# First four token tiles brought in by a transposing DMA and centred after it, in a fused layer-norm, linear-attention and gated feed-forward kernel

## The chip, the cores and the metric

The kernel runs on one core of one Trainium2 chip. The metric is the device time of one execution in microseconds; where several runs are given, their median is meant. The profile comes from one further execution, recorded by the hardware profiler. Its span goes from the first to the last instruction.

The engines are named as in the profile: PE is TensorE's matmul, PEld its weight load, DVE VectorE, ACT ScalarE, POOL GpSimd, SP SyncE. SP and ACT issue the DMAs here; the queue of SP is q1 in the profile, that of ACT is q10. 16 DMA engines serve both.

## The reference

```
x  = A_x                                   # 1 x 2048 x 640, bfloat16
xn = (x - mean(x)) / sqrt(var(x) + 1e-5)   # over the 640 columns of a token
q, k, v = split(xn @ wqkv)                 # 32 heads of 20
phi(t) = where(t > 0, t + 1, exp(t)) + 1e-6
kv  = sum over tokens of phi(k) v^T ;  z = sum over tokens of phi(k)
s   = (phi(q) kv / (phi(q) z + 1e-6)) @ wo
g   = silu(relu(xn @ w1) @ w2)             # 640 -> 1728 -> 640
out = x + s * g
```

## The kernel before, in words

The 2048 tokens are 16 tiles of 128 tokens (t = 0 to 15), or four chunks of 512 (j = 0 to 3). The 640 columns are five blocks of 128 (C = 5). A product needs its input with the columns on the partitions, so every tile of x has to be transposed. For tiles 4 to 15 that is done after the normalisation: `LN_norm` (line 487) writes the normalised tile `xn`, and `xnT_dma` (line 545) transposes it from SBUF to SBUF by a DMA of SP. Tiles 0 to 3 open the kernel and don't wait for their variance: they are only centred, transposed on TensorE, copied from PSUM into `xcT`, and multiplied; the factor 1/sqrt(var + eps) (`rsy`) is applied afterwards, as the scale of the exp and relu that empty the K products (`K_evac`, line 566).

The order of the head is written out by hand, from line 689 to line 743. Each call there appends instructions to the list of its engine, and every engine works through its own list in order. A small scheduler (`Sched`) derives the waits from what each instruction reads and writes. So an instruction that waits holds up everything behind it on its engine, whatever else is ready. The parts that matter here:

- `x_load`, `w_load`, `w1_load`, `wk_load` (lines 372 to 398) issue the loads; lines 405 to 421 are their order. x tile 0, the k part of wqkv (`wk`, five blocks of 128 rows in four loads), w1 and x tiles 4 to 7 are issued by SP, x tiles 1 to 3 by ACT.
- `fill(32)` (line 436) runs 32 products of ones with ones on TensorE from the start, `fill(5)` (line 697) five more. Their results are not used.
- `bn` (line 467) takes the statistics of half a tile on VectorE; `aggr` (line 472) joins two halves into mean and variance on VectorE, then adds eps and raises to -0.5 on POOL.
- For tiles 0 to 3 the mean comes earlier: for tiles 0 and 3 half from VectorE's half statistics (`half_mean_dve`, line 502) and half from ScalarE's accumulator (`mean_act`, line 507), for tiles 1 and 2 wholly from ScalarE. `centre` (line 514) subtracts it on VectorE, `transposes` (line 527) runs five 128x128 transposes on TensorE, and `xcT_copy` (line 534) moves the result from PSUM to `xcT` in two pieces, by VectorE or ScalarE.
- `K_mm` (line 551, matmuls at line 556) multiplies a tile of `xcT` or `xnT` by `wk`, ten matmuls of 128x320 for a tile, into two PSUM banks. `K_exp` and `K_relu` (lines 573 and 576, both at line 569) empty them on ScalarE with the scale `rsy`.
- After the four K tiles, `H_block(0, f)` for f = 4, 5, 10, 11, 12 (line 1102) multiplies blocks of w1 by all four tiles of `xcT`, five matmuls of 128x512 each (line 658), into the banks 2 to 6 in turn. The first two of these banks are those that `K_exp(0)` and `K_relu(0)` empty. Between these blocks VectorE takes the statistics of tiles 5 to 7 and normalises tiles 4 to 7.
- Then come the K products of tiles 4 to 7, the other H blocks and Q products, and a long stretch of products in Strassen form up to the output (helpers `seven` and `h_unit`, matmuls at lines 882 and 1036). None of it is touched.

Of the kernel before, what the change touches and what calls it, by code (L numbers as in the profile page):

```python
# [208 lines left out]
def bass_recurrent_scan__linear_attn_block__dense_activation_relu__prompt_kernel(  # L209
# [159 lines left out]
    def xs(t):  # L369
        return t if t < XR else (t - 4) % XR  # L370
# [20 lines left out]
    def w1_load(d0, d1, E, extra=()):  # L391
        for d in range(d0, d1):
            w_load(w1_p[d], B_w1[:, WL[d]:WL[d + 1]], ("w1", d), E=E, extra=extra)

    def wk_load(k0, k1):
        dma("SP", lambda eng: eng.dma_start(wk[:, k0:k1, :],
                                            A_wqkv[P * k0:P * k1, D:2 * D].rearrange("(c p) n -> p c n", p=P)),
            W=[("wk", k) for k in range(k0, k1)])

# [2 lines left out]
    sc.op("ACT", lambda eng: eng.activation(out=msum[:, 3, 0:1], in_=zero[:, 0:1], func=ACTF.Copy),  # L402
          R=[("zero",)], W=[("msum", 3, 0)])
    sc.allow_unread.add(("msum", 3, 0))
    x_load(0)
    x_load(1, 1, "ACT")
    wk_load(0, 1)
    x_load(2, 1, "ACT")
    wk_load(1, 2)
    x_load(3, 1, "ACT")  # L410
    wk_load(2, 3)
    wk_load(3, 5)
    w1_load(2, 3, "SP")
    w1_load(5, 6, "SP")
    x_load(4)
    x_load(5)
    w1_load(6, NW, "SP")
    x_load(6)
    x_load(7)
# [13 lines left out]
                        for _ in range(n)], W=[("ps", 7)])  # L433

    sc.allow_unread.add(("ps", 7))
    fill(32)

    def build_consts():
        sc.op("POOL", lambda eng: eng.memset(sel[:, :], 1.0 / 32), W=[("sel",)])
# [32 lines left out]
    def aggr(t):  # L472
# [12 lines left out]
    last_norm = [None]  # L485

    def LN_norm(t):
        if t >= 99:
            sc.op("POOL", lambda eng: eng.scalar_tensor_tensor(
                out=rsv[:, t:t + 1], in0=mv[:, t, 0:1], scalar=-1.0, in1=rsy[:, t:t + 1], op0=ALU.mult, op1=ALU.mult),  # L490
                R=[("mv", t), ("rsy", t)], W=[("rsv", t)])
            last_norm[0] = sc.op("ACT", lambda eng: eng.activation(
                out=xn[:, t, :], in_=xin[:, xs(t), :], func=ACTF.Identity, bias=rsv[:, t:t + 1],
                scale=rsy[:, t:t + 1]), R=[("xin", xs(t)), ("rsv", t), ("rsy", t)], W=[("xn", t)])
            xnT_dma(t)
            return
        last_norm[0] = sc.op("DVE", lambda eng: eng.tensor_scalar(
            out=xn[:, t, :], in0=xin[:, xs(t), :], scalar1=mv[:, t, 0:1], scalar2=rsy[:, t:t + 1],
            op0=ALU.subtract, op1=ALU.mult), R=[("xin", xs(t)), ("mv", t), ("rsy", t)], W=[("xn", t)])
        xnT_dma(t)  # L500

    def half_mean_dve(t):
        sc.op("DVE", lambda eng: eng.tensor_scalar(out=msum[:, t, 0:1], in0=stats[:, t, 0, 1:2],
                                                   scalar1=stats[:, t, 0, 4:5], scalar2=0.25, op0=ALU.add, op1=ALU.mult),
              R=[("stats", t, 0)], W=[("msum", t, 0)])

    def mean_act(t, lo):
        junk = ek[:, eks(t), 0, 0:D - lo]
        sc.op("ACT", lambda eng: eng.activation(out=junk, in_=xin[:, xs(t), lo:D], func=ACTF.Copy, scale=1.0 / D,
                                                accum_out=msum[:, t, 1:2]),  # L510
              R=[("xin", xs(t))], W=[("msum", t, 1), ("ek_e", eks(t))])
        sc.allow_unread.add(("ek_e", eks(t)))

    def centre(t):
        split = ((0, P * TS), (P * TS, D)) if t == 0 else ((0, D),)
        for part, (c0, c1) in enumerate(split):
            key = ("xn", t, 0) if t == 0 and part == 0 else ("xn", t)
            if t in (1, 2):
                sc.op("DVE", lambda eng, c0=c0, c1=c1: eng.tensor_scalar(
                    out=xn[:, t, c0:c1], in0=xin[:, t, c0:c1], scalar1=msum[:, t, 1:2], scalar2=None,  # L520
                    op0=ALU.subtract), R=[("xin", t), ("msum", t, 1)], W=[key])
            else:
                sc.op("DVE", lambda eng, c0=c0, c1=c1: eng.tensor_scalar(
                    out=xn[:, t, c0:c1], in0=xin[:, t, c0:c1], scalar1=msum[:, t, 0:1], scalar2=msum[:, t, 1:2],
                    op0=ALU.subtract, op1=ALU.subtract), R=[("xin", t), ("msum", t, 0), ("msum", t, 1)], W=[key])

    def transposes(t, b):
        for part, (c0, c1) in enumerate(((0, TS), (TS, C))):
            psb = ps[b + part].bitcast(bf)
            sc.group("PE", [(lambda eng, c=c, c0=c0, psb=psb: eng.transpose(  # L530
                psb[:, P * (c - c0):P * (c - c0 + 1)], xn[:, t, P * c:P * (c + 1)], ident[:])) for c in range(c0, c1)],
                R=[("xn", t, 0) if t == part == 0 else ("xn", t), ("ident",)], W=[("ps", b + part)])

    def xcT_copy(t, b, part, E):
        psb = ps[b + part].bitcast(bf)
        c0, c1 = (0, TS) if part == 0 else (TS, C)
        dst = xcT[:, c0:c1, tok(t)]
        src = psb[:, 0:P * (c1 - c0)].rearrange("p (c q) -> p c q", c=c1 - c0)
        if E == "DVE":
            sc.op("DVE", lambda eng: eng.tensor_copy(dst, src), R=[("ps", b + part)], W=[("xcT", t, part)])  # L540
        else:
            sc.op("ACT", lambda eng: eng.activation(out=dst, in_=src, func=ACTF.Copy), R=[("ps", b + part)],
                  W=[("xcT", t, part)])

    def xnT_dma(t):
        dma("SP", lambda eng: eng.dma_start_transpose(
# [139 lines left out]

    bn(0, 0)
    mean_act(0, HN)  # L690
    half_mean_dve(0)
    centre(0)
    mean_act(1, 0)
    transposes(0, 0)
    xcT_copy(0, 0, 0, "DVE")
    centre(1)
    fill(5)
    K_mm(0, 2, 0, 1)
    transposes(1, 6)
    xcT_copy(0, 0, 1, "DVE")  # L700
    mean_act(2, 0)
    xcT_copy(1, 6, 0, "DVE")
    bn(0, 1)
    xcT_copy(1, 6, 1, "ACT")
    K_mm(0, 2, 1, KA)
    K_mm(1, 4, 0, KA)
    K_mm(0, 2, 2, 3)
    centre(2)
    transposes(2, 0)
    mean_act(3, HN)  # L710
    bn(3, 0)
    xcT_copy(2, 0, 0, "DVE")
    xcT_copy(2, 0, 1, "ACT")
    half_mean_dve(3)
    centre(3)
    aggr(0)
    bn(2, 0)
    K_mm(1, 4, 2, 3)
    K_mm(2, 6, 0, KA)
    K_mm(2, 6, 2, 3)  # L720
    transposes(3, 0)
    bn(1, 0)
    xcT_copy(3, 0, 0, "DVE")
    xcT_copy(3, 0, 1, "ACT")
    bn(1, 1)
    aggr(1)
    K_mm(0, 2, 3, C)
    K_mm(1, 4, 3, C)
    bn(2, 1)
    aggr(2)  # L730
    K_exp(0, 2)
    K_relu(0, 2)
    K_mm(2, 6, 3, C)
    K_mm(3, 0)
    K_exp(1, 4)
    K_relu(1, 4)
# [960 lines left out]
```

## Time and profile before

| | us |
|---|---|
| median of 3 runs (lowest to highest) | 208.31 (208.11 to 208.32) |
| span of the profiled execution | 207.0 |
| the runs' median less that span | 1.3 |
| TensorE busy | 203.6 |
| VectorE busy | 169.7 |
| ScalarE busy | 124.3 |
| POOL busy | 18.0 |
| first matmul of the H blocks in the chain | 12.58 |

The page gives no time for the profiled execution but its span. How to read what follows: the page's first section gives for each engine its busy time, its share of the span and its instructions; the fourth the chain of work that ended last, followed back from the last instruction. The trace answers further questions: the chain in order of time, the instructions of a stretch in order of time, the busy time of each engine in given stretches, one source line's instructions, and for the DMAs the bytes that each queue moved in a stretch and the time from an issue to the landing of its last byte.

The loads of the head, issue to landing, by that last view: x tile 0 is issued by SP at 0.80 us and needs 2.5 us; x tile 1, by ACT at 0.97 us, 2.7 us; the last load of `wk` (320 KB), by SP at 2.68 us, 5.2 us; the first w1 loads (320 KB each), by SP from 3.16 us, 6.1 us.

### The profile page before, as it was taken

Reading aid. Unit: us, or ns where it says so; the run is one execution under the profiler, and the core shown is the slowest. Engines: PE = TensorE matmul, PEld = TensorE weight load, DVE = VectorE, ACT = ScalarE, POOL = GpSimd, SP = SyncE. Lnnn points to the kernel's source line nnn. Section 1 sums busy time; section 2 is a strip of 40 time slices with the busy share of each in tenths; the row PEclk is TensorE's granted clock in tenths of the full one; section 3 lists DMA queues with packets and bytes.
Section 4 is the critical chain, followed back from the end, with each engine's and each line's share of the span. In section 5 each row is a group of like instructions: output and inputs, shape, how many; then the busy total and the mean of one; then the engine's idle time right before and its main releaser. Section 6 shows DMA issues by size and latency. Waiting matters only on the chain.

```text
span 207.0 us, 3745 instructions
## 1 busy us (share of the span) xinstructions
PE 203.6 (98%) x1400; PEld 126.3 (61%) x1400; DVE 169.7 (82%) x373; ACT 124.3 (60%) x251; POOL 18.0 (9%) x53
## 2 busy tenths in 40 slices
PE   8999999999999999999999999999999999999995
PEld 7755645545555444444456777777777777777773
DVE  4888997988969787686889669898888989897465
ACT  5598869888889987686563435462525354352531
POOL 3174032101330000000000000000000000000001
PEclk9999999999999999999999999999999999999999
DMA  6965999211037000302225999237931011010103
GB/s 194 331 190 117 255 203 275 42 32 29 6 63 198 25 3 0 127 0 57 74 63 114 251 357 384 90 108 234 371 129 63 3 63 46 21 63 0 63 5 127
DMA packets 32999, 24.74 MB, mean 119 GB/s; under 512 B 12757, under 2 KB 32981, under 8 KB 32981
## 3 DMA queue, kind: packets, MB, share of 16 engines
q1 hardware_dynamic: 31749, 23.13, 39.2%
q10 hardware_dynamic: 1232, 1.37, 1.9%
q8 instruction: 11, 0.18, 0.4%
q14 instruction: 7, 0.06, 0.1%
HBM read 15.81 MB, written 5.24 MB: 102 GB/s over the span
## 4 chain that ended last, share of the span: by engine, by line
PE 97%; DMA 1%; DVE 1%; issue 0%
PE psT L882 40%; PE psT L1036 19%; PE psT L556 11%; PE psT L609 11%; PE psT L658 6%; PE psT L1529 3%; PE psT L1580 2%; DMA reg<-in_A_x_dram 1%; PE psT L676 1%; PE psT L1320 1%; PE psT L530 1%; PE psT L1294 1%; PE psT L756 1%; PE psT L786 1%; PE psT L432 0%; DVE stats L469 0%
## 5 line engine op out<-in xcount | busy, mean ns | idle before, releaser
L882 PE MATMUL psT<-reg,regH 128*128 128x320 bf16 (+1 forms) x224 | 34.3, 299 | 0.0
L882 PE MATMUL psT<-reg 128*128 128x320 bf16 (+1 forms) x164 | 27.7, 299 | 0.0
L882 PEld LDWEIGHTS psT<-reg,regH 128*128 128x128 bf16 (+1 forms) x224 | 21.9, 98 | 8.6
L1354 ACT ACTIVATE wv_sb<-psT 128x320 bf16<-128x320 f32 x28 | 11.3, 436 | 25.2 <-PE psT L882 15.4
L609 PE MATMUL psT<-reg 128*128 128x512 bf16 x100 | 24.4, 379 | 0.0
L1036 PE MATMUL psT<-reg 128*128 128x512 bf16 x80 | 23.2, 379 | 0.0
L827 DVE TENSOR_TENSOR psT<-psT,reg 128x320 f32<-128x320 f32 x30 | 14.3, 493 | 9.3 <-PE psT L882 9.2
L889 ACT ACTIVATE psT<-psT 128x320 f32<-128x320 f32 x32 | 13.6, 426 | 11.2 <-PE psT L882 10.7
L882 PEld LDWEIGHTS psT<-reg 128*128 128x128 f16 (+1 forms) x164 | 16.0, 98 | 6.9 <-DVE regH L827 0.2
L889 ACT ACTIVATE reg<-psT 128x320 f32<-128x320 f32 (+1 forms) x24 | 10.4, 435 | 15.6 <-PE psT L882 13.6
L556 PE MATMUL psT<-reg 128*128 128x320 bf16 x120 | 17.9, 299 | 0.0
L1042 ACT ACTIVATE psT<-psT 128x512 f32<-128x512 f32 x20 | 11.9, 595 | 8.2 <-PE psT L1036 8.2
L569 ACT ACTIVATE regE<-psT 128x640 bf16<-128x640 f32 x24 | 15.6, 706 | 1.9 <-PE psT L556 1.2
L609 PEld LDWEIGHTS psT<-reg 128*128 128x128 bf16 x100 | 9.6, 98 | 11.6 <-issue 0.7
L1048 ACT ACTIVATE regH<-psT 128x512 bf16<-128x512 f32 (+1 forms) x24 | 14.5, 604 | 2.1 <-PE psT L1036 1.8
L556 PEld LDWEIGHTS psT<-reg 128*128 128x128 bf16 x120 | 11.5, 98 | 6.5 <-ACT regE L569 0.5
L469 DVE BATCH_NORM_STATS2 stats<-reg 128x6 f32<-128x320 bf16 x32 | 14.1, 475 | 1.3 <-DMA reg<-in_A_x_dram 1.3
L827 DVE TENSOR_TENSOR reg<-reg 128x1024 f16<-128x1024 bf16 (+6 forms) x17 | 13.5, 805 | 1.7 <-DMA reg<-in_B_w_dram 1.2
L882 PE MATMUL psT<-reg,pqT 128*128 128x320 bf16 (+1 forms) x72 | 14.7, 299 | 0.0
L1517 DVE TENSOR_TENSOR reg<-psT,wv_sb 128x640 bf16<-128x640 f32 (+2 forms) x16 | 11.8, 739 | 3.0 <-PE psT L882 1.8
L1036 PEld LDWEIGHTS psT<-reg 128*128 128x128 bf16 x80 | 7.7, 98 | 9.4 <-issue 0.4
L1522 POOL TENSOR_TENSOR reg<-reg 128x224 bf16<-128x224 bf16 x1 | 0.6, 607 | 144.0 <-DVE reg L1517 144.0
(143 smaller groups left out, 369.0 us busy)
## 6 DMA issues: line engine op xcount, KB each, us to landing
reg<-in_B_w_dram SPq DMA_DIRECT2D x12, 320.0 KB, 5.5
scr<-rden SPq DMA_DIRECT2D x4, 640.0 KB, 8.3
reg<-in_A_x_dram SPq DMA_DIRECT2D x4, 640.0 KB, 6.6
out_dram<-reg SPq DMA_DIRECT2D x15, 160.0 KB, 1.9
regE<-scr SPq DMA_DIRECT2D x3, 640.0 KB, 7.5
reg<-in_A_x_dram SPq DMA_DIRECT2D x4, 320.0 KB, 4.4
reg<-in_A_wo_dram SPq DMA_DIRECT2D x6, 160.0 KB, 3.3
reg<-in_A_x_dram SPq DMA_DIRECT2D x5, 160.0 KB, 5.5
```

The lines of the kernel that those rows point to most:

```text
L469: sc.op("DVE", lambda eng: eng.bn_stats(stats[:, t, a, :], xv[:, HN * a:HN * (a + 1)]), R=[("xin", xs(t))], W=[("stats", t, a)])
L556: fns.append(lambda eng, a=a, k=k, lhs=lhs: eng.matmul(ps[b + a][:, 0:HN], lhsT=lhs, rhs=wk[:, k, HN * a:HN * (a + 1)], start=(k == 0), st ...
L569: sc.op("ACT", lambda eng: eng.activation(out=o_.rearrange("p (a n) -> p a n", a=2), in_=ps2(b, HN), func=func, scale=scale), R=[("ps", b) ...
L609: sc.group("PE", [(lambda eng, k=k: eng.matmul(ps[b], lhsT=wq[:, k, P * f:P * (f + 1)], rhs=xnT[:, j, k, :], start=(k == 0), stop=(k == C ...
L658: sc.group("PE", [(lambda eng, k=k: eng.matmul(ps[b], lhsT=w1_col(k, P * f, P), rhs=src[:, k, :], start=(k == 0), stop=(k == C - 1))) for ...
L827: sc.op("DVE", lambda eng: eng.tensor_tensor(out=out, in0=in0, in1=in1, op=op), R=R, W=W, extra=extra)
L882: sc.group("PE", [(lambda eng, k=k, lhs=lhs, rhs=rhs: eng.matmul(ps[b][:, 0:HN], lhsT=lhs, rhs=rhs, start=(start and k == 0), stop=(k == n ...
L889: sc.op("ACT", lambda eng: eng.activation(out=dst, in_=ps[b][:, 0:HN], func=ACTF.Copy), R=[("ps", b)], W=[dkey], extra=extra)
L1036: sc.group("PE", [(lambda eng, k=k, lhs=lhs, rhs=rhs: eng.matmul(ps[b], lhsT=lhs, rhs=rhs, start=(start and k == 0), stop=(k == n - 1), sk ...
L1042: sc.op("ACT", lambda eng: eng.activation(out=dst, in_=ps[b], func=ACTF.Copy), R=[("ps", b)], W=[dkey], extra=extra)
L1048: sc.op("ACT", lambda eng: eng.activation(out=dst, in_=ps[b], func=ACTF.Relu), R=[("ps", b)], W=[("hT", j, f)])
L1517: sc.op("DVE", lambda eng: eng.tensor_tensor(out=tmpo[:, os_, lo:hi].rearrange(shp, a=na), in0=src, in1=g_of(t)[0][:, lo:hi].rearrange(shp ...
```

## The change

The raw tiles 0 to 3 of x come twice. Once they come by a DMA that transposes on the way, straight from DRAM into `xcT` (`xT_load`, issued by SP ahead of all else); once as before into `xin`, for the statistics and the later normalisation. On the transposed tile the mean of a token is a sum over partitions: `sums` multiplies ones by the five blocks, so that each row of the PSUM tile holds the token sums, and the new `centre` subtracts sum/640 on VectorE, in place, in two pieces. The transposes, the copies and the early means of before are gone. The variances of tiles 0 and 1 move to ScalarE (`act_stats`: a pass for the mean, a pass of squares); those of tiles 2 and 3 stay with VectorE. ACT now issues all loads of `wk` and of x tiles 0 to 3, the last two in one; on SP, x tiles 4 and 5 go ahead of a w1 block. The fillers are 29 and 3.

```diff
-    def wk_load(k0, k1):
-        dma("SP", lambda eng: eng.dma_start(wk[:, k0:k1, :],
+    def wk_load(k0, k1, E="SP"):
+        dma(E, lambda eng: eng.dma_start(wk[:, k0:k1, :],
...
-    x_load(0)
+    def xT_load(t):
+        dma("SP", lambda eng: eng.dma_start_transpose(xcT[:, :, tok(t)], x2[tok(t), :]), W=[("xr", t)])
+
+    for t in range(4):
+        xT_load(t)
+    wk_load(0, 1, "ACT")
+    wk_load(1, 2, "ACT")
+    wk_load(2, 3, "ACT")
+    wk_load(3, 5, "ACT")
+    x_load(0, 1, "ACT")
     x_load(1, 1, "ACT")
-    wk_load(0, 1)
-    x_load(2, 1, "ACT")
-    wk_load(1, 2)
-    x_load(3, 1, "ACT")
-    wk_load(2, 3)
-    wk_load(3, 5)
+    x_load(2, 2, "ACT")
     w1_load(2, 3, "SP")
-    w1_load(5, 6, "SP")
     x_load(4)
     x_load(5)
+    w1_load(5, 6, "SP")
     w1_load(6, NW, "SP")
...
-    fill(32)
+    fill(29)
...
+    def act_stats(t):
+        junk = ek[:, eks(t), 0, :]
+        key = ("ek_e", eks(t))
+        sc.allow_unread.add(key)
+        sc.op("ACT", lambda eng: eng.activation(out=junk, in_=xin[:, t, :], func=ACTF.Copy, scale=-1.0 / D,
+                                                accum_out=msum[:, t, 0:1]), R=[("xin", t)], W=[("msum", t, 0), key])
+        sc.op("ACT", lambda eng: eng.activation(out=junk, in_=xin[:, t, :], func=ACTF.Square, bias=msum[:, t, 0:1],
+                                                accum_out=msum[:, t, 1:2]),
+              R=[("xin", t), ("msum", t, 0)], W=[("msum", t, 1), key])
+        sc.op("POOL", lambda eng: eng.tensor_scalar(out=rsv[:, t:t + 1], in0=msum[:, t, 1:2], scalar1=1.0 / D,
+                                                    scalar2=EPS_LN, op0=ALU.mult, op1=ALU.add),
+              R=[("msum", t, 1)], W=[("rsv", t)])
...
-        if t >= 99:
...
+        if t < NA:
+            last_norm[0] = sc.op("DVE", lambda eng: eng.tensor_scalar(
+                out=xn[:, t, :], in0=xin[:, t, :], scalar1=msum[:, t, 0:1], scalar2=rsy[:, t:t + 1],
+                op0=ALU.add, op1=ALU.mult), R=[("xin", t), ("msum", t, 0), ("rsy", t)], W=[("xn", t)])
...
+    def sums(t, b):
+        sc.group("PE", [(lambda eng, c=c: eng.matmul(ps[b][:, 0:P], lhsT=one, rhs=xcT[:, c, tok(t)],
+                                                     start=(c == 0), stop=(c == C - 1))) for c in range(C)],
+                 R=[("xr", t)], W=[("ps", b)])
+
+    def centre(t, b, part):
         c0, c1 = (0, TS) if part == 0 else (TS, C)
...
+        o_ = xcT[:, c0:c1, tok(t)]
+        sc.op("DVE", lambda eng: eng.scalar_tensor_tensor(
+            out=o_, in0=ps[b][:, 0:P].unsqueeze(1).to_broadcast([P, c1 - c0, P]), scalar=-1.0 / D, in1=o_,
+            op0=ALU.mult, op1=ALU.add), R=[("ps", b), ("xr", t)], W=[("xcT", t, part)])
```

`NA` is 2. The head's order before is lines 689 to 733 above; after the change it reads, up to the K products of tile 3 and from there on as before:

```
    sums(0, 0)
    centre(0, 0, 0)
    centre(0, 0, 1)
    fill(3)
    act_stats(0)
    K_mm(0, 2, 0, KA)
    K_mm(0, 2, 2, 3)
    sums(1, 1)
    centre(1, 1, 0)
    centre(1, 1, 1)
    K_mm(0, 2, 3, C)
    act_stats(1)
    K_mm(1, 4, 0, KA)
    sums(2, 0)
    bn(2, 0)
    centre(2, 0, 0)
    centre(2, 0, 1)
    K_mm(1, 4, KA, C)
    K_exp(0, 2)
    K_relu(0, 2)
    bn(2, 1)
    K_mm(2, 6, 0, KA)
    sums(3, 1)
    centre(3, 1, 0)
    centre(3, 1, 1)
    K_mm(2, 6, KA, C)
    aggr(2)
    bn(3, 0)
    K_mm(3, 0)
```

More of the change, by code (lines that the diff above doesn't have):

```diff
@@ L379, in w_load @@
         dma(E, lambda eng: eng.dma_start(dst, src.rearrange("(c p) n -> p c n", p=P)), W=[key], extra=extra)
+    NA = 2
     KA = 2
@@ L478, in aggr @@
                                                     op=ALU.pow), R=[("rsv", t), ("mhalf",)], W=[("rsy", t)])
+    def act_stats(t):
[10 more added lines that the diff above has]
+              R=[("msum", t, 1)], W=[("rsv", t)])
+        sc.op("POOL", lambda eng: eng.tensor_tensor(out=rsy[:, t:t + 1], in0=rsv[:, t:t + 1], in1=mhalf[:, :],
+                                                    op=ALU.pow), R=[("rsv", t), ("mhalf",)], W=[("rsy", t)])
     def LN_stats(t):
@@ L487, in LN_norm @@
     def LN_norm(t):
-        if t >= 99:
[L489 to L494, printed above, removed]
+        if t < NA:
+            last_norm[0] = sc.op("DVE", lambda eng: eng.tensor_scalar(
+                out=xn[:, t, :], in0=xin[:, t, :], scalar1=msum[:, t, 0:1], scalar2=rsy[:, t:t + 1],
+                op0=ALU.add, op1=ALU.mult), R=[("xin", t), ("msum", t, 0), ("rsy", t)], W=[("xn", t)])
             xnT_dma(t)
@@ L500, in LN_norm @@
         xnT_dma(t)
[L502 to L535, printed above, removed]
-        c0, c1 = (0, TS) if part == 0 else (TS, C)
[L537 to L543, printed above, removed]
+    def sums(t, b):
+        sc.group("PE", [(lambda eng, c=c: eng.matmul(ps[b][:, 0:P], lhsT=one, rhs=xcT[:, c, tok(t)],
+                                                     start=(c == 0), stop=(c == C - 1))) for c in range(C)],
+                 R=[("xr", t)], W=[("ps", b)])
@@ L685, in H_half @@
         return a
[L689 to L705, printed above, removed]
-    K_mm(1, 4, 0, KA)
[L707 to L716, printed above, removed]
-    bn(2, 0)
[L718 to L730, printed above, removed]
+    sums(0, 0)
[4 more added lines that the diff above has]
+    K_mm(0, 2, 0, KA)
+    K_mm(0, 2, 2, 3)
+    sums(1, 1)
+    centre(1, 1, 0)
+    centre(1, 1, 1)
+    K_mm(0, 2, 3, C)
+    act_stats(1)
+    K_mm(1, 4, 0, KA)
+    sums(2, 0)
+    bn(2, 0)
+    centre(2, 0, 0)
+    centre(2, 0, 1)
+    K_mm(1, 4, KA, C)
     K_exp(0, 2)
     K_relu(0, 2)
-    K_mm(2, 6, 3, C)
+    bn(2, 1)
+    K_mm(2, 6, 0, KA)
+    sums(3, 1)
+    centre(3, 1, 0)
+    centre(3, 1, 1)
+    K_mm(2, 6, KA, C)
+    aggr(2)
+    bn(3, 0)
     K_mm(3, 0)
```

## The prediction, made before the changed kernel was run

> **What bounds the kernel now.** I read the page first: shares by engine, then the chain that ended last.
>
> ```profile
> PE 203.6 (98%) x1400; PEld 126.3 (61%) x1400; DVE 169.7 (82%) x373; ACT 124.3 (60%) x251; POOL 18.0 (9%) x53
> ...
> PE 97%; DMA 1%; DVE 1%; issue 0%
> ```
>
> TensorE is busy 98% of the span and is 97% of the chain; the rest lies at the two ends. So whatever shifts the first unbroken stretch of TensorE work shifts the end by the same amount, unless a later wait swallows it. The change touches only the head, so the second view is the chain in order of time, 0 to 40 us (columns: start, length, what):
>
> ```profile
> 0.80 2.48 DMA reg<-in_A_x_dram
> ...
> 4.49 0.79 PE psT L530 x5
> 5.28 0.53 PE psT L432 x5
> 5.81 0.52 PE psT L556 x2
> 6.33 0.28 PE psT L530 x5
> 6.61 1.21 PE psT L556 x8
> ...
> 9.59 2.99 PE psT L556 x22
> 12.58 5.40 PE psT L658 x25
> ```
>
> From 4.49 us TensorE never stops: transposes (L530), filler (L432), K products (L556), and at 12.58 the first H products (L658). The mark to compare is that **12.58**. The K products before 6.2 us take 0.26 us each, later 0.15 and 0.136 us: the array is at half rate until about 6.2 us (the 32 fillers, 0.84 to 4.41 us, give 0.112 us each, against 0.056 for the transposes at 6.33). The clock column below shows 1.00 there too; I go by the durations.
>
> Third, what the transfers do meanwhile: stretches of 1 us (last two columns: DMA share, GB/s) and the queues in 3 to 4 us (packets, MB, share):
>
> ```profile
> 3.00:4.00 1.00, 1.00 (x13) 1.00 (x11) 0.66 (x2) 0.70 (x3) 0.15 (x1) 1.00 0.99 341
> 7.00:8.00 1.00, 1.00 (x12) 0.81 (x11) 0.89 (x4) 0.68 (x3) 0.00 (x0) 1.00 1.15 339
> ```
>
> ```profile
> q1 hardware_dynamic: 147, 0.17, 50.8%
> q10 hardware_dynamic: 153, 0.17, 48.5%
> ```
>
> The DMA engines are **full** from 2 us on: two queues together move 341 GB/s, one alone 339. So an early byte that is added delays every later byte, and moving loads to ACT's queue (q10) buys no rate. Over 1.9 to 8 us the mean is 320 GB/s.
>
> **The change, part by part.**
>
> TensorE: 20 transposes go and 20 products with ones of the same 128x128 shape come, so nothing at full rate (0.056 us each); fillers fall from 37 to 32. Gain: the first K product no longer waits for statistics, half mean, centring, transposes and a copy (3.30 to 5.6 us). The new head is 29 fillers to 0.84 + 29 x 0.112 = 4.1, five sums at half rate 0.56, one centring 0.42: K starts at 5.1 instead of 5.8. Until 6.2 that gives 1.1/0.26 = 4 K products instead of 1.5; the 2.5 more are worth 2.5 x 0.136 = 0.35 us. With all waits gone the H mark would be 6.2 + 36 x 0.136 + 15 x 0.056 = 11.9. The gain cannot pass 0.65 us.
>
> VectorE: four half statistics (0.47), two aggregations and two half means (0.21), five centrings (1.9 in all) and five copies (1.5) go: 6.2 us. Eight centrings from PSUM come. The trace has no such form (PSUM read broadcast, bf16 in and out). Nearest row:
>
> ```profile
> L1517 DVE TENSOR_TENSOR reg<-psT,wv_sb x16: 374/822/825, 144.5 to 204.5; 128x640 bf16<-128x640 f32 x13, 128x208 bf16<-128x208 f32 x2, 128x224 bf16<-128x224 f32 x1
> ```
>
> 208 to 640 columns go from 0.374 to 0.822 us, about 1.04 ns a column: 0.42 for 256 and 0.56 for 384, in a row some 0.37 and 0.50 (two statistics in a row take 0.83, not 0.94). Low bound: the PSUM copies removed, 0.29 and 0.35; high bound 0.42 and 0.56. I take 0.37 + 0.50.
>
> ScalarE: four mean passes (0.46 to 0.74), their accumulator reads (0.19) and three copies (0.48) go, 4.6 us; four passes over 640 columns with reads (0.73 + 0.19) come, 3.7 us. But they stand in order before the first exp: x0 and x1 in, 1.8 us each, then exp and relu (0.7 each) free the banks that the first H product needs. If x0 lands at 8 and x1 by 9, the banks are free at 8 + 3.6 + 1.4 = 13.0. POOL keeps its two small operations a tile (0.85) behind these.
>
> DMA: four transposing loads from DRAM are added, x0 to x3 stay, so their bytes move twice. What a transposing load from DRAM costs, no row shows; these move SBUF to SBUF:
>
> ```profile
> 14.58 5.57 SPq L546 DMA_TRANSPOSE reg<-reg  x4
> ```
>
> ```profile
> DMA packets 1956, 0.48 MB, mean 251 GB/s; under 512 B 1956, under 2 KB 1956, under 8 KB 1956
> ```
>
> The first is SP's queue in the timeline: 1.2 to 1.3 us to issue one, and in quiet 2.7 us to landing. The second is the DMA view over 26.35 to 28.26 us, when transposes ran back to back: 1956 packets, three tiles, in 1.91 us, 0.64 us a tile with all engines full. A plain tile of 164 KB at 320 GB/s is 0.51. Bounds for a tile of the new kind: 0.51, and 1.25 (SP's issue). I take 0.64, the nearest full row.
>
> [...] The row here gives 251 GB/s. [...]
>
> Now the queue. ACT issues wk (four loads), x0, x1, then x2 and x3 as one load, from 0.97 us, seven at 0.45: the last leaves at 4.1. SP's transposes leave at 0.8, 2.05, 3.3, 4.6. The first lands at about 3.6 (0.8 + 2.7 and a little for DRAM): in time for the fillers' end. All nine plain tiles (1.47 MB) and the four transposes are 4.6 + 4 x 0.64 = 7.2 us of full DMA from 1.9: done at **9.1**. What can raise it: before, the load that ended the same 1.47 MB (320 KB of wk, issued 2.68, 5.2 to landing) landed at 7.9, where 1.9 + 4.6 is 6.5. So up to 1.4 for lagging engines; and w1's first block, on SP behind the transposes (issued about 6), shares the last stretch. I put x2/x3 at X = 9.8; bounds 8.5 (tiles at 0.51, no lag) and 11 (9.1 + 1.4 + half a microsecond of w1).
>
> **Who waits for X:** VectorE's statistics of tile 2, bn(2,0), stand in its order *before* the centring of tile 2. Queued behind that wait are centre(2), bn(2,1) and centre(3), so K(2) and K(3), though their transposes are long in. From X: bn 0.42, centre(2) 0.87, bn 0.42, centre(3) 0.87, latencies 0.1, then K(3), 10 x 0.136 (K(2) lies beside centre(3)): 4.1 us. H mark: 9.8 + 4.1 = **13.9**, against 12.58. TensorE ends K(1) at about 9 and stands until centre(2), 11.1. ScalarE's banks (13.0, or 13.9 with the lag on x0 too) are a near second.
>
> Behind that: N4 comes at X + 5.9 (aggregations, POOL), its transposed tile 2.7 + 0.45 later at 18.9, and the H block ends at 13.9 + 5.4 = 19.3: covered, by 0.4. w1, x4, x5 leave SP two us later than before; their 0.65 MB need 2 us more at 320 GB/s, so they are in by 12.5 even with the lag, and are wanted from 13.4 (bn of tile 4) and 13.9. So +1.3 stays to the end. The span goes from 207.0 to 208.3. The runs' median, 208.31, is 1.3 above the span of the profiled execution, whose own time the page does not give otherwise; I carry that over: **209.6 us**.
>
> **Rivals.**
>
> 1. *Not slower: the plain loads get ahead.* If the queues take turns load by load and SP needs 1.25 us an issue, ACT's loads may pass the transposes, and X fall to 8.5 or less: the point from which it decides (8.5 + 4.1 = 12.6; up to 8.9 no run could tell). At the other end tile 3's transpose must land by 9.8 (sums 0.3, centring 0.95, K(3) 1.4). Then the mark is 11.9 to 12.8. For it: the even shares of q1 and q10. Against it: the lag. 207.7 to 208.6, likely 208.2.
> 2. *The transposes from DRAM are dear*, at 1.25 us of DMA each: X later by 2.4, also the case where the change does not do what it says, as the raw tiles then come later than centred ones did. +3.7, 212.0; half of that 210.8.
> 3. *The clock stays at half.* A hole before tile 0's transpose keeps the array slow through K(3): K(2) and K(3) cost 2.6 each, +2.6, 212. In the trace full rate came at 6.2 after unbroken work.
>
> [...]
>
> **How the numbers follow.** Forecast (X from 8.9 to 11): 0.52, giving 208.7 to 210.8. First rival 0.30, of which 0.13 below 207.9. Dear transposes 0.11, slow clock 0.07. A difference under 0.2%, 0.42 us, is about what a measurement of this kernel cannot tell from none: faster 0.13, same 0.17, slower 0.70. The range, 207.7 to 211.3, leaves out most of the last two cases (0.13) and little below.
>
> **What would show it.** In the changed profile: L658's first product near 13.9; a TensorE hole of about 2 us before tile 2's K products; VectorE's bn(2,0) waiting for x, released near 9.8, beside transposes already in; the x2/x3 load with 5.5 us or more from issue to landing; centrings of 0.4 to 0.55 us. I am wrong if bn(2,0) never waits, or if the hole is there and a later stage takes it back.

## The result, and the profile after the change

The changed kernel takes **214.91 us** (median of 6 runs, 214.21 to 216.03), the kernel before 208.31 beside it (6 runs, 207.62 to 208.42): 1.0302 times as long, 95% interval 1.0267 to 1.0337, or 6.6 us slower. The forecast was 209.6, slower, with a range of 207.7 to 211.3. The direction was right; the size was five times the 1.3 us forecast. The profiled execution's span is 213.4 us, 6.4 above before's 207.0.

From the page of after, busy time by engine and shares of the chain that ended last:

```profile
PE 204.7 (96%) x1395; PEld 126.9 (59%) x1395; DVE 167.7 (79%) x363; ACT 124.0 (58%) x248; POOL 18.2 (9%) x53
...
PE 85%; DVE 6%; DMA 5%; issue 1%; POOL 1%; SPq 1%
```

TensorE has 1.1 us more busy time, VectorE 2 us less, yet the span grew by 6.4: TensorE now stands still. Its share of the chain fell from 97% to 85%, and DVE and DMA have come in. Where that happens is read from the chain in order of time, 0 to 45 us (start, length, what):

```profile
2.19 7.96 DMA regX<-in_A_x_dram
10.21 0.72 PE psT L520 x5
10.92 2.13 PE psT L542 x8
13.05 0.53 PE psT L520 x5
13.59 1.90 PE psT L542 x10
15.49 0.29 PE psT L520 x5
15.81 0.89 DVE regX L527 x2
...
31.93 3.43 DMA reg<-reg
35.35 0.09 issue
35.44 1.26 PE psT L662 x20
```

(L520 are the sums, L542 the K products, L527 the centrings, L662 the half H block.) The first line is the load to look at: the transposing load of tile 1, issued by SP at 2.19, lands at 10.16, 8 us later. The sums of tile 1 begin the moment it is in. TensorE's own stops stand in the timeline (start, length, what, in brackets the idle time before it and what ended that):

```profile
5.93 0.45 PE L520 MATMUL psT<-regX,const-bfloat16-1.0 128*128 128x128 bf16 x5 [1.84 <-DMA regX<-in_A_x_dram]
...
10.21 0.72 PE L520 MATMUL psT<-regX,const-bfloat16-1.0 128*128 128x128 bf16 x5 [2.29 <-DMA regX<-in_A_x_dram]
...
18.12 5.56 PE L644 MATMUL psT<-regX,reg 128*128 128x512 bf16 x25
...
35.44 1.26 PE L662 MATMUL psT<-reg 128*32 128x512 bf16 x20 [0.51 <-DMA reg<-reg]
```

The H mark, the first L644 product, is **18.12**. By the timeline, which is read from here on, it was 12.41 before (the chain cuts it at 12.58, where the product ahead of it ends): 5.7 us later. TensorE's holes up to it are 1.84, 0.35, 2.29 and 0.17, together 4.65; the other 1.1 is longer work, at half rate. At the half H block (before at 29.16, now 35.44) another hole of 0.51 has come in. From the first Q product on, both kernels take the same: 176.7 us before, 176.8 after. So all of the loss lies ahead of it, 5.7 at the H mark and 0.6 at 35 us.

What the transfers do meanwhile: stretches of 2 us of after (length, busy us of PE, PEld, DVE, ACT, POOL, granted clock, DMA share, GB/s):

```profile
4.00:6.00 2.00, 0.16 (x3) 0.07 (x2) 0.00 (x0) 0.00 (x0) 0.00 (x0) 1.00 1.18 132
6.00:8.00 2.00, 1.57 (x14) 0.88 (x14) 0.89 (x2) 0.00 (x0) 0.00 (x0) 0.93 0.98 143
8.00:10.00 2.00, 0.00 (x0) 0.00 (x0) 0.00 (x0) 0.00 (x0) 0.00 (x0) 0.50 1.13 204
10.00:12.00 2.00, 1.79 (x10) 1.27 (x11) 0.89 (x2) 1.80 (x5) 0.00 (x0) 0.50 1.29 300
```

The DMA share reads full, but the last column says that the engines move **132 and 143 GB/s**; before it was 307 and 348 in the same stretches. No engine computes from 8 to 10 us, and the clock falls to half. Now the queues, 4 to 8 us, in the DMA view of after (packets, MB, share of 16 engines):

```profile
q10 hardware_dynamic: 333, 0.40, 71.0%
q1 hardware_dynamic: 611, 0.15, 36.8%
```

and of before in the same stretch:

```profile
q1 hardware_dynamic: 1500, 1.12, 87.0%
q10 hardware_dynamic: 174, 0.19, 15.1%
```

Share x 16 engines x 4 us, over the packets: a plain packet of 1.2 KB on ACT's queue (q10) takes 136 ns in after; before, one of about the same size on the same queue (1.1 KB) takes 56 ns. So the plain loads are the ones that became slow, while transposes of SP (q1) stand beside them. The landings follow: raw tiles 0 to 3 at 5.89, 10.16, 11.81 and 13.31; `wk` complete at 9.65 (before 7.88); x2/x3 at 12.71.

### The profile page after: what moved, and what is told of

Same layout as the page of the kernel before. It is cut to its first block, busy times and chain, and to the rows that moved or that the text cites. A ratio compares the mean times of both kernels' runs of the same rounds, so it can differ in the third digit from the quotient of the medians.

```text
span 213.4 us, 3722 instructions
## 1 busy us (share of the span) xinstructions
PE 204.7 (96%) x1395; PEld 126.9 (59%) x1395; DVE 167.7 (79%) x363; ACT 124.0 (58%) x248; POOL 18.2 (9%) x53
## 3 DMA queue, kind: packets, MB, share of 16 engines
q10 hardware_dynamic: 2064, 2.35, 4.4%
## 4 chain that ended last, share of the span: by engine, by line
PE 85%; DVE 6%; DMA 5%; issue 1%; POOL 1%; SPq 1%
PE psT L851 39%; PE psT L1005 18%; PE psT L595 10%; PE psT L542 7%; DMA regX<-in_A_x_dram 4%; PE psT L1498 2%; DVE stats L474 2%; PE psT L1549 2%; DMA reg<-reg 2%; PE psT L662 1%; PE psT L644 1%; PE psT L1289 1%; DVE reg L514 1%; PE psT L520 1%; DVE regE L571 1%
## 5 line engine op out<-in xcount | busy, mean ns | idle before, releaser
L542 PE MATMUL psT<-reg 128*128 128x320 bf16 x120 | 17.9, 299 | 0.0
L542 PEld LDWEIGHTS psT<-reg 128*128 128x128 bf16 x120 | 11.6, 98 | 6.4 <-ACT regE L555 0.5
L474 DVE BATCH_NORM_STATS2 stats<-reg 128x6 f32<-128x320 bf16 x28 | 12.3, 476 | 0.9 <-DMA reg<-in_A_x_dram 0.9
L603 ACT ACTIVATE regE<-psT 128x512 bf16<-128x512 f32 x20 | 12.0, 601 | 1.5 <-PE psT L595 1.5
```

The lines of the kernel that those rows point to most:

```text
L474: sc.op("DVE", lambda eng: eng.bn_stats(stats[:, t, a, :], xv[:, HN * a:HN * (a + 1)]), R=[("xin", xs(t))], W=[("stats", t, a)])
L542: fns.append(lambda eng, a=a, k=k, lhs=lhs: eng.matmul(ps[b + a][:, 0:HN], lhsT=lhs, rhs=wk[:, k, HN * a:HN * (a + 1)], start=(k == 0), st ...
L603: sc.op("ACT", lambda eng: eng.activation(out=e_, in_=ps[b], func=ACTF.Exp), R=[("ps", b)], W=[("er_e", es)])
```

## The experiments

The theory after the result (A): transposing and plain loads hold each other up in the DMA engines, and that alone makes the head late. Its rivals: (B) a transposing load from DRAM is dear by itself; (C) the raw tiles come late because a second queue takes half the engines and the bytes come twice, whatever the kind of load; (D) the half clock; (E) VectorE's order, as the prediction had it. Medians in us, with the ratio to the kernel before on the same chip; the H mark is the start of the first H product in the timeline. Each H mark is that of one profiled execution: two profiles of the same kernel lie 1.1 us apart (c3, c3b) and 0.7 (e6, e6b), so differences of that size between H marks show little. In e1, e2, e3, e6, c0, c1 and c2 the trace has 24 of the 25 H products, and the mark can be one product, 0.2 us, late.

| kernel | us | ratio, 95% | H mark |
|---|---|---|---|
| before | 208.31 | 1 | 12.41 |
| after | 214.91 | 1.030, 1.027 to 1.034 | 18.12 |
| e1_plain | 213.41 | 1.024, 1.022 to 1.027 | 16.13 |
| e2_one_queue | 214.76 | 1.031, 1.030 to 1.033 | 17.89 |
| e3_held | 220.15 | 1.057, 1.053 to 1.061 | 22.65 |
| e4_bn_behind | 215.23 | 1.030, 1.024 to 1.037 | 17.21 |
| e5_warm | 217.98 | 1.048, 1.045 to 1.051 | 16.70 |
| e6_x_held | 219.13 | 1.050, 1.046 to 1.054 | 23.60 |
| e7_grouped | 216.23 | 1.034, 1.028 to 1.040 | 20.22 |
| e8_x_held_plain | 219.13 | 1.054, 1.047 to 1.061 | 23.24 |
| e6b_x_held | 219.75 | 1.057, 1.041 to 1.072 | 24.26 |
| c0_act_loads | 212.45 | 1.020, 1.016 to 1.023 | 15.52 |
| c1_spare_plain | 212.89 | 1.021, 1.016 to 1.026 | 17.59 |
| c2_spare_transposed | 213.35 | 1.022, 1.018 to 1.027 | 17.95 |
| c3_w1_held | 211.07 | 1.010, 1.006 to 1.013 | 13.14 |
| c3b_control | 212.03 | 1.012, 1.003 to 1.020 | 14.28 |
| c4_plain256 | 212.61 | 1.017, 1.010 to 1.024 | 16.09 |
| c5_transposed | 212.60 | 1.017, 1.009 to 1.025 | - |
| g1_compute_side | 212.36 | 1.016, 1.009 to 1.023 | 16.06 |

### The same bytes, not transposed: e1

```diff
-        dma("SP", lambda eng: eng.dma_start_transpose(xcT[:, :, tok(t)], x2[tok(t), :]), W=[("xr", t)])
+        dma("SP", lambda eng: eng.dma_start(xcT[:, :, tok(t)], x2[tok(t), :].rearrange("p (c q) -> p c q", c=C)), W=[("xr", t)])
```

> The four transposing loads are replaced by plain loads of the same tiles into the same places in the same 256-byte pieces (x stands untransposed there, so the K and H products of the first chunk multiply other numbers). Theory A (transposes on SP's queue and plain loads on ACT's hold each other up inside the DMA engines): the stall from 5 to 8 us goes, the raw tile 0 lands by 4, the x2/x3 load by 10, the H mark comes at 13 to 14 and the time falls to 208.5 to 210. Theory C (simply more bytes in small pieces): landings and time stay as in the changed kernel, about 214.9. Theory B (a transposing load from DRAM is slow by itself) expects the same as A here.

213.41 us: 1.5 us under after, not 5. In the stretches the DMA moves 327 GB/s from 6 to 8 us, where after moves 143, so the mutual slowing is real; but from 4 to 5.5 it is still only 194. The raw tiles land at 4.19, 8.31, 9.12 and 10.78, x2/x3 at 11.66. TensorE still waits for raw tile 1, this time 1.19 us, and the clock falls to half again (0.52 in the mean from 8 to 10 us). So A alone fell: **most of the loss is there without any transposing.**

But e1 changes more than the kind of load. SP issues its four plain loads in 3.3 us, the four transposes in 5.95, so w1 and tile 4 of x follow sooner and come in ahead of x2/x3. The DMA view of after from 1.9 us to the landing of x2/x3 (12.71), and of e1 likewise (11.66):

```profile
DMA packets 4061, 2.19 MB, mean 202 GB/s; under 512 B 2800, under 2 KB 4061, under 8 KB 4061
```

```profile
DMA packets 4898, 2.77 MB, mean 284 GB/s; under 512 B 2768, under 2 KB 4898, under 8 KB 4898
```

In after the bytes are those that were forecast (2.13 MB) and the rate is low; in e1 the rate is nearly back, but 0.58 MB more have moved by the time x2/x3 are in. At e1's 284 GB/s the 2.19 MB would be in by 9.6, an estimate. So the 1.5 us are what is left after one loss took the other's place, and no upper bound for what the mixing costs.

### Transposes by themselves: e3

```diff
-    for t in range(4):
-        xT_load(t)
-    wk_load(0, 1, "ACT")
+    raw = [xT_load(t) for t in range(4)]
+    wk_load(0, 1, "ACT", raw)
...
-    w1_load(2, 3, "SP")
+    w1_load(2, 3, "SP", raw)
```

> ACT's seven loads and SP's first w1 load wait until all four transposes have landed: the transposes from DRAM run alone. Theory A: they land 2.7 to 3 us after their issue, 1.3 apart, at about 3.6, 4.9, 6.2 and 7.5; the rest comes 6 us later than in the changed kernel's issue order, so the time itself is 214 to 217 and says little. Theory B: each lands 4 us or more after its issue, the last after 9.

The time, 220.15 for 214 to 217 expected, only says that the plain loads came 5 to 7 us late. The landings are the point: 3.68, 5.11, 6.51, 7.95, each about 3 us after its issue and 1.4 apart, with the issues 1.3 apart. Timeline and stretch of e3 (in the second: length, busy times, clock, DMA share, GB/s):

```profile
0.80 5.28 SPq L407 DMA_TRANSPOSE regX<-in_A_x_dram  x4
```

```profile
2.00:8.00 6.00, 2.94 (x28) 2.68 (x26) 0.92 (x3) 0.29 (x2) 1.01 (x4) 1.00 0.54 109
```

Alone, four transposes keep the engines busy half the time (0.54) and wait for SP to issue them. Raw tile 1 is in at 5.11, where after gets it at 10.16. So B is refuted: the transpose is dear only in company.

### The order on one queue, and in groups: e2, e7

In e2 all early loads go through SP, in the order of need (`xT0, wk0-2, xT1, wk3-4, x0, xT2, x1, xT3, x2/x3`); in e7 through SP too, the four transposes first:

```diff
     for t in range(4):
         xT_load(t)
-    wk_load(0, 1, "ACT")
...
+    wk_load(0, 1)
...
```

> All the early loads are issued by SP, in the order xT0, wk 0 to 2, xT1, wk 3-4, x0, xT2, x1, xT3, x2/x3, so that transposes and plain loads stand in one queue. Theory A: no stall, xT0 lands near 3.6, xT1 near 6, x2/x3 by 11.5 to 12 (SP's issue is the limit), H mark near 15 to 16, time 210.5 to 212. Theory B: xT1 lands 2 us or more after its issue would allow and the time stays at 214 or above.

> The changed kernel with all early loads on SP, the four transposes first and together, then wk and x: one change between the kinds in place of many. If the changes stall, the raw tiles land at 3.6, 5, 6.4 and 7.8, x2/x3 by 12.5, the H mark is 15 to 16.5 (ScalarE's variances of x0 and x1 come last) and the time 211 to 213.5, below 214.9 although wk now waits behind all transposes. If bytes alone count, nothing is won: 214.5 or more.

Neither helps: 214.76 and 216.23. In e2 three stretches around a change of kind moved 74, 39 and 140 GB/s (DMA share and GB/s last):

```profile
3.00:4.00 1.00, 1.00 (x13) 1.00 (x11) 0.00 (x0) 0.00 (x0) 0.15 (x1) 1.00 0.62 74
6.50:7.00 0.50, 0.50 (x3) 0.30 (x2) 0.00 (x0) 0.00 (x0) 0.00 (x0) 1.00 0.92 39
10.50:11.50 1.00, 1.00 (x8) 0.77 (x7) 0.00 (x0) 1.00 (x3) 0.22 (x2) 1.00 0.86 140
```

In e7 there is one such change, but the transposes alone are slow to issue (1.3 us each in e3; 132 GB/s from 4 to 8 us) and `wk` is complete only at 12.68: the H mark is 20.22. Mixed, separated by queue or separated in time, the raw tiles plus the plain loads don't fit into the time before they are needed. Its expectation, 211 to 213.5, was a miss. In e2, 214 or more was the sign given for (B); the landings of e3 speak against that reading.

Part of such a stretch may be the start of a load as such: the first plain packets of the kernel before, from 1.75 to 2.25 us, come at 148 GB/s only.

### The kind of load, with little else in flight: e6, e6b, e8

x0 to x3 wait here until the raw tiles are in; `wk` is in flight beside those and, behind them on SP, w1 and later tiles of x. e6 and e6b are the same kernel with transposes, e8 has plain loads in 256-byte pieces in their place (as e1).

```diff
-    x_load(0, 1, "ACT")
+    x_load(0, 1, "ACT", raw)
```

> The changed kernel with ACT's loads of x0 to x3 held until the four transposes have landed; wk still runs beside them. Tests what the second load of x costs the first tiles. If bytes decide, the four raw tiles land 1.5 to 2 us earlier (xT1 by 8.5, xT3 by 11.5), but x0 comes at 14 and the first exp waits for its statistics, so the H mark is 17 to 18.5 and the time 213.5 to 215.5. If the mixing with wk is the whole stall, xT1 lands after 9.5 as before.

> The changed kernel with x0 to x3 held back, and the four raw tiles loaded plain in 256-byte pieces (untransposed, so the first chunk multiplies other numbers): only wk and the raw tiles are in flight, 1.46 MB, 4.6 us at 320 GB/s. If transposing beside plain loads is what slows the DMA engines, they move 290 GB/s or more from 4 to 6.5 us here and the fourth raw tile lands by 7.5, against 10.2. If two queues with 256-byte pieces are slow in any form, it lands after 9.

> The same with transposing loads, once more on the same chip: 140 to 220 GB/s from 4 to 8 us, raw tiles at 5 to 6, 8.5 to 9.5, 9 to 10 and 9.7 to 10.7.

The times (219.13, 219.13, 219.75) say nothing here, since the late x0 to x3 hold the statistics up. What is compared is the DMA rate, the last column of the stretches. e8, plain:

```profile
4.00:6.00 2.00, 1.27 (x10) 0.90 (x10) 0.63 (x2) 0.00 (x0) 0.00 (x0) 1.00 0.90 254
6.00:8.00 2.00, 1.90 (x8) 0.57 (x7) 0.26 (x1) 0.00 (x0) 0.00 (x0) 1.00 1.19 307
```

e6b, transposing:

```profile
4.00:6.00 2.00, 0.88 (x10) 0.66 (x11) 0.74 (x2) 0.00 (x0) 0.00 (x0) 1.00 0.85 125
6.00:8.00 2.00, 0.89 (x6) 0.23 (x3) 0.15 (x1) 0.00 (x0) 0.00 (x0) 1.00 1.17 219
```

Same sources, same bytes, same queues: 125 and 219 GB/s with transposes, 254 and 307 without, at nearly the same DMA share. e6 gave 157 and 201. The second raw tile lands at 9.37 for 7.82, the fourth at 10.47 for 9.26. This is the cleanest pair for the mutual slowing; it is worth 1.2 to 1.6 us of landing time. But it isn't all: e8's own expectation was 290 GB/s and the fourth raw tile by 7.5 if the kind of load were the whole matter, and a landing after 9 if two queues with 256-byte pieces are slow in any form. It landed at 9.26. In e6 the raw tiles 1 and 3 land at 9.11 and 10.22 (after: 10.16 and 13.31), tile 1 between what its expectation gave to bytes (8.5) and to mixing (9.5 or later). Its time, 213.5 to 215.5 expected, was a miss.

### The queues alone: c0, c3, c3b

The kernel before, with x0 to x3 and `wk` all issued by ACT, so that SP begins with w1; in c3 and c3b w1 also waits for the third `wk` load.

```diff
-    x_load(0)
+    x_load(0, 1, "ACT")
...
-    wk_load(0, 1)
+    wk_load(0, 1, "ACT")
...
```

> The kernel before, with nothing changed but the queue of its early loads: x0 to x3 and all of wk are issued by ACT in their old order, SP begins with w1. Control for the next two. If the queue alone matters, wk's last load (landed 7.9 before) comes 1 to 2 us later, because w1 now runs beside it from the start, and the time is 209 to 210; if not, 208.3.

> The control with all early loads on ACT, with SP's w1 held until ACT's third wk load has landed, so that nothing runs beside ACT's queue before. If the two queues shared the DMA engines evenly and that made the control slow (212.45), x0 lands by 3.3 again, the last wk by 8.5, and the time is 208.3 to 209.5. If ACT's queue is slow by itself, it stays at 211 or more.

> The control with w1 held, once more on the same chip as the next two: H mark near 13.1, time 209.3 to 211.3.

c0 is **4.1 us slower than before with no byte added**: 212.45, where 209 to 210 was expected. Its queues, 4 to 8 us, in the DMA view:

```profile
q1 hardware_dynamic: 1171, 0.74, 62.7%
q10 hardware_dynamic: 545, 0.63, 48.3%
```

Both queues move about the same, at a full 343 GB/s together. SP's 0.74 MB is w1 and later tiles of x, which nobody needs yet, and ACT's x and `wk` get the other half: x0 lands at 4.18 (before 3.28), the last `wk` load at 11.73 (before 7.88), the H mark is 15.52. With w1 held back the H mark is 13.14 and the time 211.07 (10 runs, 209.26 to 211.61); repeated on another chip, where before itself took 209.19, 14.28 and 212.03.

So holding w1 back returns 2.4 of c0's 3.1 us at the H mark (1.2 by c3b), but only 1.4 of its 4.1 us in the medians: c3 stays 2.4 us above before (208.64 beside it), where 208.3 to 209.5 was expected. By its expectation 211 or more spoke for a slow queue of ACT, but its landings (x0 at 3.26, `wk` complete at 8.33) don't show one. The two profiles of this kernel say where the rest can come from. c3's is of a quick execution (209.51), c3b's of a long one (212.86). By the time of a K product the array reaches full rate at 6.2 us in c3 and at 8.9 in c3b, with the H mark 1.14 later; and in c3b the half H block waits 1.98 us for transposed tiles, in c3 not at all. By the half H block c3b is 2.9 of the 3.35 us behind; what decides the two is open.

So (C) is shown in part, for before's kernel. In after the shares aren't even: from 4 to 8 us SP's queue moved 0.15 MB of 0.55. Nor are they in e1, whose pieces on SP have 256 bytes (5.5 to 8 us, DMA view):

```profile
q10 hardware_dynamic: 464, 0.54, 60.9%
q1 hardware_dynamic: 1004, 0.25, 44.8%
```

There the queue with the short pieces got a third of the bytes, with 318 GB/s in total, and raw tile 1 landed at 8.31.

By what the DMA engines divide themselves between two queues, no run here shows: c0's two rows have about equal bytes (0.74 and 0.63 MB) and not equal numbers of what the profile calls packets (1171 and 545), e1's have neither. That the split doesn't go by need, both show.

### Spare loads of both kinds on before's kernel: c1, c2, c4, c5

c0 with four extra loads of x0 to x3 ahead on SP, whose result nobody reads: plain in c1, transposing in c2. c4 and c5 are the same on top of c3; c4's go to a strided target and so move in 256-byte pieces. (c1's pieces came out at 1280 bytes, so c1 is no 256-byte control.)

```diff
+    for t in range(4):
+        spare_load(t)
     x_load(0, 1, "ACT")
```

> The control with four more loads ahead on SP: x0 to x3 once more, plain, in 256-byte pieces, into space that nobody reads. Theory 1 (the added bytes cost, whatever their form): 0.66 MB at 320 GB/s is 2 us of full DMA, of which some only takes w1's place: the last wk lands 1 to 2.5 us after the control's and the time is 1 to 2.5 us above it. Theory 2 (only transposing hurts): as the control, within 0.5.

> The same four spare loads, transposing. Theory 1: as the plain ones, within 0.7, since 640 packets of 256 bytes a tile move in either case. Theory 2 (transposes beside plain loads stall the DMA engines): a stretch under 200 GB/s between 4 and 8 us, the last wk 2 us or more behind the plain variant, time 1.5 to 3 us above it.

> That control with four spare loads of x0 to x3 ahead on SP, plain, in true 256-byte pieces; w1 stays behind, so that only these run beside ACT's queue. If the bytes are the larger part, the last wk lands 1.5 to 2.5 us after the control's, the DMA engines move 300 GB/s or more from 2.5 to 9 us, and the time is 1.5 to 2.5 us above the control.

> The same four spare loads, transposing. If changing between transposes and plain loads stalls the DMA engines, they move 140 to 240 GB/s from 4 to 9 us, the last wk lands 2 us or more after that of the plain variant, and the time is 2 us or more above it. If it is bytes alone, both are alike.

The rates repeat the pair above. c1, 4 to 8 us:

```profile
4.00:8.00 4.00, 1.88 (x21) 1.17 (x19) 2.18 (x9) 1.57 (x5) 0.00 (x0) 0.97 1.05 331
```

c2, the same stretch:

```profile
4.00:8.00 4.00, 1.78 (x21) 1.17 (x19) 1.64 (x7) 1.28 (x4) 0.00 (x0) 1.00 1.13 175
```

The last `wk` load lands at 11.86 in c1 and 12.98 in c2. But the times, 212.89 and 213.35, can't be told apart, nor from c0's 212.45 with confidence; 212.61 (c4) and 212.60 (c5) can't either. So c1 is within 0.5 of its control, which was given to transposing alone, but c2 is not the 1.5 to 3 us above c1 that went with it; c4 missed its 1.5 to 2.5 above its control (212.03), c5 its 2 or more above c4. In c4 the last `wk` load landed at 10.92, 2.5 after the control's, as expected of the added bytes. The H marks do move with the added bytes, 15.52 to 17.59 and 17.95, and the end takes most of it back: c0 has a hole of 1.88 us ahead of the half H block and c2 has none. c5 has no H mark here: its profiled execution took 216.08 us, 3.5 above its median.

### The clock: e5

```diff
-    fill(29)
+    fill(45)
...
     K_mm(0, 2, 2, 3)
+    fill(40)
     sums(1, 1)
```

(the second filler stands ahead of the sums of tile 1, so that TensorE has work in the hole)

> The changed kernel with fillers in its two TensorE holes (45 in place of 29 at the start, 40 more ahead of the sums of tile 1), so that the array is not idle. If the half clock (7.7 to 14.6 us) is what costs, the H mark comes 1 to 2 us earlier and the time falls to 213 to 214. If the transfers alone decide, the time stays within 0.5 of 214.9, since TensorE only waits at full rate instead of at half rate.

The clock stays full from 5.21 through the head and the H mark comes at 16.70, 1.4 us earlier than in after. Of these 1.4, 0.6 stand beside an earlier landing of raw tile 1 (9.53 for 10.16). Yet the kernel is slower than after, 217.98, outside both branches of its expectation. Two stretches of e5 (granted clock, DMA share and GB/s last):

```profile
33.30:35.65 2.35, 0.00 (x2) 0.03 (x1) 0.55 (x3) 0.60 (x1) 0.79 (x2) 1.00 1.33 201
35.93:39.34 3.41, 3.19 (x23) 1.04 (x17) 3.38 (x7) 1.18 (x2) 0.00 (x0) 0.50 1.14 335
```

TensorE gets to the half H block earlier, finds the transposed tiles missing, stands for 2.35 us and then falls to half clock. So, by these two profiles, (D) costs up to 0.8 us at the H mark, and that gain would not have reached the end by itself.

The clock column doesn't show every stretch at half rate. In e4 below it reads 1.00 from 10 to 12 us, but eight K products take 2.34 us from 10.16 on, as in after at 0.50; by their time the array first reaches full rate at 13.3 in e4, at 6.0 in after.

### VectorE's order: e4

```diff
     sums(2, 0)
-    bn(2, 0)
     centre(2, 0, 0)
...
-    bn(2, 1)
...
     K_mm(2, 6, KA, C)
+    bn(2, 0)
+    bn(2, 1)
     aggr(2)
```

> The changed kernel with the two half statistics of tile 2 moved behind the centrings of tiles 2 and 3 in VectorE's order. By the prediction (VectorE's wait for x2/x3 holds tiles 2 and 3 back) the H mark comes 0.9 us or more earlier and the time falls to 214 or less. By the traces so far (the raw tiles themselves are late, and TensorE is at half rate) nothing changes: 214.5 to 215.3.

215.23 us, ratio 1.0302, as after. Centre(2) now waits for the sums alone, and the H mark is 17.21 (raw tile 1 also landed 0.56 earlier in that profile); the end does not move. The chain of e4 in order of time says why:

```profile
15.78 0.81 DVE stats L474 x2
...
31.98 3.42 DMA reg<-reg
35.40 0.09 issue
35.49 1.26 PE psT L662 x20
```

From 15.8 us it is VectorE, not TensorE: statistics and normalisation of tile after tile, and at 31.98 the transpose of the last of the normalised tiles 0 to 3, which lands at 35.40; in after the same link starts at 31.93 and lands at 35.35. So **a second chain sets the half H block**: it leaves TensorE at the last centring and runs beside the H blocks, and an H mark that is 0.9 earlier only makes the hole larger (1.01 us in e4 for 0.51). In e5 this chain comes out of VectorE 1.2 us earlier, and the transposes take it back, 4.87 us for 3.43:

```profile
30.69 4.87 DMA reg<-reg
35.56 0.09 issue
35.65 1.63 PE psT L662 x13
```

### The compute side alone: g1

Loads as before; the raw tile is transposed on TensorE, copied, and then summed and centred as in after.

```diff
+    raw_T(0, 0)
...
     sums(0, 0)
...
```

> The change without its transfers: loads as in the kernel before; the raw tiles are transposed on TensorE and copied to xcT, then summed with ones and centred there, variances as in the change. 15 sums more at 0.056 us are 0.84 us of TensorE beside the transposes, the first K product comes about when it did. If the transfers are the cause, H mark 13 to 14 and time 208.8 to 210. If the new centring or ScalarE's variances cost by themselves, 212 or more.

212.36 us, against an expectation of 208.8 to 210. The profile shows holes of 0.95, 0.60 and 0.98 us in TensorE that wait for VectorE's copies and centrings: in my order transposes, copies, sums and centring of a tile follow each other. By its expectation 212 or more would mean that the new centring or ScalarE's variances cost by themselves, but g1 adds a chain that neither kernel has, and so does not isolate what it was made for. The compute side is not excluded by it. In after, the waits of TensorE for the centrings are 0.35 and 0.17 us of the 4.65 ahead of the H mark.

No version beat the kernel before, and none of the runs pointed to one that would.

## Why the prediction was right and where it was wrong

- **What bounds it, right for the kernel before.** TensorE's unbroken head sets the end there, and the DMA is full from 2 us on. After the change the chain leaves TensorE at 15.8 us, and 0.6 of the 6.3 us lost ahead of the first Q product comes at the half H block, behind the head.
- **"All nine plain tiles and the four transposes are 4.6 + 4 x 0.64 = 7.2 us of full DMA from 1.9: done at 9.1", and so X = 9.8: this is the step that failed.** X was 12.71, beyond the upper bound of 11. The bytes were right, the rate was not: from 1.9 us to 12.71 the engines moved 2.19 MB, 2.13 forecast, at 202 GB/s, where 7.2 us for 2.13 MB would be 296. I priced each load by what it does among its own kind, plain ones at 320 GB/s and transposes at 251 back to back, and added the two. In company the engines moved 138 GB/s over 4 to 8 us. That the company of the two kinds lowers the rate is shown (e6b and e8: 125 against 254 GB/s). How much of the 6.6 us it makes is not: without transposes (e1) the time falls by 1.5 us only, but w1 then comes in ahead of x2/x3. Nor did I price loads in 256-byte pieces beside longer ones, and a second queue whose loads nobody needs yet (c0: +4.1 us with no byte added).
- **"The first lands at about 3.6": it landed at 5.89.** Alone it does land at 3.68 (e3). The 2.2 us in between come with the plain loads beside it (other profiles with the same early loads have 4.92 in e5 and 5.08 in e4): TensorE ran out of fillers at 4.09 and stood 1.84 us. K started at 6.90, forecast 5.1.
- **"X + 4.1" by VectorE's bn(2,0): wrong as mechanism.** The wait is there, 0.88 us, but the chain does not go through it: it runs from raw tile 1 over TensorE to the centring of tile 3, ahead of which VectorE is idle for 0.89 us. Without that wait (e4) the H mark is 0.9 earlier, 0.55 of which stand beside an earlier raw tile 1, and the time is the same. TensorE waits earlier and for something else: raw tile 1, 2.29 us before 10.21. From X to the H mark it took 5.4 us in after, 4.5 in e5, where the array was at full rate. I let "their transposes are long in" stand without pricing SP's second transpose in company; it took 8 us.
- **Rival 3, the clock, was given 0.07 and happened**, though not as written: the hole before tile 0 did not keep the array slow, it came to full rate at 6.0 us and lost it from 7.74 to 14.57. That cost up to 0.8 us at the H mark (e5), not 2.6. The clock column of after reads 1.00 from 4.33 to 7.74 and 0.50 from there: in these 3.41 us ahead of the fall TensorE was idle for 1.95 us and worked for 1.46.
- **"Covered, by 0.4": right, but not the last cover.** The sum was for tile 4 and the first H blocks: in after its transposed tile lands at 22.84, and the K products that need it start at 23.52. "So +1.3 stays to the end" left out the next one, at the half H block. There the last transposed tile landed at 28.87 for 29.16 before. After, it landed at 35.35, and TensorE was ready at 34.94. The H mark's 5.7 would have brought it in at 34.6; 0.8 came on top, against 0.3 of cover, which leaves the hole of 0.5. Seen beside it, from 33.2 to 34.0, the DMA engines moved almost nothing between the transposes of tiles 0 and 1 (12 GB/s), just after an instruction fetch at 32.7. e5 shows a similar standstill (6 GB/s from 31.5 to 32.5). That the fetch is the cause was not tested.
- **Rival 2, dear transposes, refuted** (e3). **Rival 1, plain loads ahead of the transposes:** they did not get ahead: `wk` was complete at 9.65 instead of 7.88, and x2/x3 at 12.71, where the rival needed 8.5.
- **The small terms held.** Centring took 0.89 us a tile, forecast 0.87. TensorE's work changed by little, and the span and the median moved together (6.4 and 6.6).

A sign of it was in the trace of before: after its first four transposes of xn the next plain load begins slowly. Its stretch from 21 to 22 us (DMA share and GB/s last):

```profile
21.00:22.00 1.00, 1.00 (x10) 0.68 (x7) 0.97 (x4) 1.00 (x2) 0.00 (x0) 1.00 0.51 58
```

58 GB/s. Not all of it is a change of kind: the load was issued at 20.19 and its first packet starts at 21.44. But over the half microsecond from 21.4 it gives 74 GB/s, where the first load of the kernel gives 148 over its first half (1.75 to 2.25).

Open: how much of the 6.6 us falls to the transposes in company, to the queue beside them, to the doubled bytes and to the short pieces, which the runs don't separate cleanly (e1 takes the transposing away and lets w1 in; c0 and c1 differ by 2 us at the H mark and by 0.4 in time); why the loads dip to 194 GB/s at 4 to 5.5 us in e1; what decides when the array first comes to full rate (6.2 us in c3, 8.9 in c3b); and the cause of the standstill at 33 us.

## What to carry to other kernels

Price an added load in its place among the others, not by its rate alone: with `wk` ahead of w1 on one queue its last load landed at 7.88 us (before), with w1 on the other queue at 11.73, as that queue took its share of the same DMA engines, needed or not (0.74 MB beside 0.63 in c0). The transposing DMA, quick alone (5.11 us for raw tile 1 in e3, 10.16 in after), slowed the plain loads beside it (136 ns a packet in after, 56 in before), so check GB/s, not the DMA share, in a stretch of the trace where both kinds meet. Before counting a gain, look for the second chain that ends where the first one does.

## What the runs showed of the hardware that was not expected

- The DMA share reads 1.0 to 1.2 while the engines move 132 to 143 GB/s (after, 4 to 8 us), with a plain packet of 1.2 KB taking 136 ns in the mean; in c0, without transposes, one of the same size took 57 ns (48.3% of 16 engines over 4 us, 545 packets).
- In e2, with all early loads on one queue, stretches of half a microsecond to one around a change between transposes and plain loads moved 39 to 140 GB/s.
- The clock column misses the first stretch at half rate: by the times of the matmuls the array came to full rate at 6.0 us in after, 6.2 in c3, 8.9 in c3b (the same kernel) and 13.3 in e4, while the column of e4 reads 1.00.
- TensorE's granted clock stood at half for 6.83 us in after (7.74 to 14.57) and for 3.41 in e5 (35.93 to 39.34), and the 3.41 us ahead of a fall were idle only in part: 1.89 us of them in e1, 1.95 in after and 2.35 in e5 (33.30 to 35.65). In e8 the column still reads 1.00 from 10 to 12 us, where TensorE was idle for 0.73 us.
- The transposing loads from DRAM, alone, landed about 3 us after their issue each (0.80 to 3.68 us for the first), and 1.4 us apart, with SP's issues 1.3 us apart (e3).
